# Two heads in one 32x32 product for the block between an inverse's halves

## The chip, the cores and the metric

The kernel runs on one core of one Trainium2 chip. The metric is device time in microseconds (us) for one whole execution. The engines are named as the profile names them: PE is TensorE's matrix multiply and PEld its weight load, DVE is VectorE, ACT is ScalarE, POOL is GpSimd, and SP is the engine that issues every DMA of this kernel.

## What is computed

The reference has two parts. The first is a recurrence over 768 time steps for 4 batches of 8 heads, each head with a 40x40 state. The second is a feed-forward layer over the 3072 tokens `x` that come out of it, from 320 columns to 2048 and back.

```
for t in range(S):
    ...
    y[:, :, t] = np.einsum('bhd,bhde->bhe', rt, state)
    Sa = np.einsum('bhde,bhe->bhd', state, at)
    state_decay = state * wt[:, :, None, :] - np.einsum('bhd,bhe->bhde', Sa, bt)
    state = state_decay + np.einsum('bhd,bhe->bhde', vt, kt)
...
h = x @ w_in
sp = np.maximum(h, 0.0) + np.log1p(np.exp(-np.abs(h)))
g = h * erf(sp)
return (g @ w_out).astype(np.float32)
```

## The kernel before

**Chunks and supersteps.** Time is cut into chunks of 32 steps. Inside a chunk the 32 steps of one head are solved together, which needs the inverse of a unit triangular 32x32 matrix per head and chunk. Heads are handled in two groups of 16. A superstep is 128 time steps (4 chunks) of one group, so there are 12 supersteps, numbered 0 to 11 here, and 64 such matrices in each.

**The parts of a superstep.** `prep` loads and scans the decay factors. `aphase` (once for each chunk) builds the triangular matrices with the PE step `A`, masks them on DVE and sends them to the DRAM tile `AD`. `tphase` inverts all 64 matrices of the superstep. `chain` (once for each chunk) carries the state: its PE steps are `Z`, `U`, `pmt`, `M`, `UT`, `PQ` and `Y`, and `U` needs the inverses. The feed-forward layer of the superstep before runs beside it: `mm1` is `x @ w_in`, followed by ACT and DVE work for `erf(softplus(h))`, and `mm2` is `g @ w_out`. One `mm2` step is two matmul records of the trace, one `mm1` step is eight.

**The T-phase, which the change touches.** A 32x32 unit triangular matrix is inverted by halves. The two 16x16 diagonal blocks of every matrix are loaded into the tile `Ti` and inverted there by 28 short DVE steps (`Tm`, `Ts`). The result, the inverse D of the diagonal blocks, goes to the DRAM tile `TD` by two DMAs and comes back as the tile `Tb` by four DMAs (`tb`), with each 32x32 matrix in 32 partitions and 32 columns: four matrices stand side by side in the 128 partitions and sixteen in the columns. Beside that, four DMAs (`Ap`, 64 KB each) bring the original matrices from `AD` into the tile `Ap` in the same layout. What is missing is the 16x16 block between the two halves. It comes out of D, A and D multiplied:

- `R` (DVE, L742) transposes `Tb` in blocks of 32x32 into the tile `T`
- `W` (PE, L749, four steps of sixteen 32x32 products) multiplies `Ap` with it into the PSUM bank `pA`
- `Wm` (DVE, L753) copies the bank to `T`, masked so that only the wanted 16x16 corner of each 32x32 block is left
- `DAD` (PE, L749, four steps of sixteen products) multiplies that with `Tb`
- `Tb` (DVE, L756) adds the product to the tile `Tb`

Each product is of fp32 and is two weight loads and two matmul records in the trace, so `W` is 128 matmul records in a superstep and so is `DAD`. Afterwards `U` of the next four chunks reads `Tb`.

**What sets the order.** The class `Plan` collects every step with its reads and writes. The order in which the steps are issued, and the engine of each step that has a choice (DVE, ACT or POOL), are read from two written lists, `ORDER` and `ENGINES`. Each engine executes its steps strictly in that order and waits for what a step depends on. In `ORDER` an entry of -1 or -2 is a filler matmul (L581), used at the start and at the end. There are 241 of them. SP takes its DMAs in order as well: a DMA that waits for its data holds back those behind it. `HOLD`, `ISSUE`, `PAIRS` and `COLS` are costs for a planner that runs only when the two lists do not fit the steps.

## Time and profile before

| what | value |
|---|---|
| median of 3 runs | 821.89 us |
| lowest, highest of the 3 | 817.88 us, 829.41 us |
| the profiled execution's own time | 825.36 us |
| its span, first to last instruction | 823.4 us |
| PE busy | 760.1 us (92% of the span) |
| DVE busy | 656.6 us (80%) |
| ACT busy | 609.6 us (74%) |
| POOL busy | 142.4 us (17%) |
| mean granted PE clock | 0.956 of full |

The profile is one execution. A group line names source line, engine, operation, the tiles written and read, the shapes and a count; then the busy time in us and the mean of one in ns; then the idle time of the engine just before these instructions and what ended it. A timeline line gives start and duration in us; rows of one kind that touch are merged, with their count. The end of a matmul is modelled, so a matmul row that seems long can hold a wait, and the start of the next row is the better measure. The chain of waits follows the work that ended last back to the start.

### The profile page before, as it was taken

Reading aid. Unit: us, or ns where it says so; the run is one execution under the profiler, and the core shown is the slowest. Engines: PE = TensorE matmul, PEld = TensorE weight load, DVE = VectorE, ACT = ScalarE, POOL = GpSimd, SP = SyncE. Lnnn points to the kernel's source line nnn. Section 1 sums busy time; section 2 is a strip of 40 time slices with the busy share of each in tenths; the row PEclk is TensorE's granted clock in tenths of the full one; section 3 lists DMA queues with packets and bytes.
Section 4 is the critical chain, followed back from the end, with each engine's and each line's share of the span. In section 5 each row is a group of like instructions: output and inputs, shape, how many; then the busy total and the mean of one; then the engine's idle time right before and its main releaser. Section 6 shows DMA issues by size and latency. Waiting matters only on the chain.

```text
span 823.4 us, 32379 instructions
## 1 busy us (share of the span) xinstructions
PE 760.1 (92%) x13778; PEld 588.3 (71%) x13778; DVE 656.6 (80%) x1430; ACT 609.6 (74%) x1202; POOL 142.4 (17%) x116
## 2 busy tenths in 40 slices
PE   5845998889999999999999999999899999999997
PEld 2413667657878878878877777778678777887864
DVE  6975866877889979889887978889689788778574
ACT  5453738764987878888977877878778888798882
POOL 2200321113022003011031032022123130021100
PEclk8685999889999999999998999999999999999999
DMA  8886755576666556557555546555556365313000
GB/s 253 218 218 202 182 135 145 149 167 169 145 142 166 133 146 166 146 139 176 143 157 145 143 119 158 151 142 142 136 139 153 88 162 137 69 55 94 1 17 20
DMA packets 141666, 114.60 MB, mean 139 GB/s; under 512 B 84972, under 2 KB 121964, under 8 KB 141516
## 3 DMA queue, kind: packets, MB, share of 16 engines
q1 hardware_dynamic: 141516, 112.47, 53.6%
q8 instruction: 110, 1.80, 1.0%
q14 instruction: 40, 0.33, 0.1%
HBM read 86.47 MB, written 22.02 MB: 132 GB/s over the span
## 4 chain that ended last, share of the span: by engine, by line
PE 76%; DVE 7%; DMA 6%; ACT 4%; issue 4%; SPq 1%; DVEq 0%; ACTq 0%
PE po L1067 25%; PE ph L1012 19%; PE pA L749 4%; PE gb L856 4%; PE cb L829 4%; PE pA L688 3%; PE pQ L847 3%; PE ph L581 3%; PE cb L805 2%; PE cb L796 2%; PE pQ L817 2%; PE pA L703 2%; PE gb L838 1%; PE pQ L581 1%; SPq L578 1%
## 5 line engine op out<-in xcount | busy, mean ns | idle before, releaser
L1067 PE MATMUL po<-wo,h 128*128 128x320 f32 x768 | 254.8, 456 | 1.3 <-issue 0.7
L1067 PEld LDWEIGHTS po<-wo,h 128*128 128x128 f32 x768 | 134.8, 193 | 42.5 <-issue 3.6
L1020 ACT ACTIVATE l<-l 128x512 f32<-128x512 f32 x192 | 112.2, 626 | 10.6 <-DVE nd L1045 10.1
L1012 PE MATMUL ph<-xh,wih 128*128 128x256 f32 x384 | 89.5, 314 | 0.3 <-ACT h L573 0.3
L678 POOL TENSOR_TENSOR Ab<-bk,Pr 104x512 f32<-104x512 f32 x25 | 32.9, 1318 | 275.0 <-PE pA L688 153.1
L1012 PE MATMUL ph<-xh,wil 128*128 128x256 f32 x384 | 77.4, 283 | 0.0
L1012 PE MATMUL ph<-xl,wih 128*128 128x256 f32 x384 | 77.4, 283 | 0.0
L1057 POOL TENSOR_TENSOR l<-l,r 128x512 f32<-128x512 f32 x32 | 45.2, 1420 | 174.7 <-ACT l L1020 75.3
L1058 DVE SCALAR_TENSOR_TENSOR h<-l,h 128x512 f32<-128x512 f32 x96 | 66.4, 701 | 4.4 <-POOL l L1057 2.2
L1046 DVE SCALAR_TENSOR_TENSOR r<-nd,r 128x512 f32<-128x512 f32 x96 | 66.5, 693 | 1.6 <-POOL nd L1045 0.2
L1020 ACT ACTIVATE l<-h 128x512 f32<-128x512 f32 x96 | 58.1, 627 | 12.2 <-DVE h L1058 6.0
L1012 PEld LDWEIGHTS ph<-xh,wih 128*128 128x128 f32 x384 | 61.1, 191 | 7.2 <-ACT h L573 0.4
L1045 DVE TENSOR_TENSOR nd<-l,r 128x512 f32<-128x512 f32 x76 | 53.6, 706 | 9.5 <-ACT r L1020 6.0
L1012 PEld LDWEIGHTS ph<-xh,wil 128*128 128x128 f32 x384 | 59.9, 192 | 0.0
L1012 PEld LDWEIGHTS ph<-xl,wih 128*128 128x128 f32 x384 | 59.7, 191 | 0.0
L581 PE MATMUL ph<-d 104*128 104x512 bf16 x183 | 54.2, 439 | 4.9 <-DVE d L593 4.9
L653 DVE TENSOR_TENSOR Zs<-pA,tri 64x256 f32<-64x256 f32 x96 | 40.6, 423 | 21.0 <-PE pA L688 17.7
L1020 ACT ACTIVATE r<-r 128x512 f32<-128x512 f32 x96 | 56.7, 625 | 0.5
L1020 ACT ACTIVATE r<-l 128x512 f32<-128x512 f32 x96 | 54.1, 619 | 2.8 <-DVE l L1057 1.5
L573 ACT COPY Zm<-cb 32x160 f32<-32x160 f32 x127 | 35.8, 282 | 26.7 <-PE cb L805 18.3
L1012 PE MATMUL ph<-xl,wir 128*128 128x256 f32 x192 | 54.4, 283 | 0.0
L1012 PE MATMUL ph<-xh,wir 128*128 128x256 f32 x192 | 54.3, 283 | 0.0
(135 smaller groups left out, 1528.1 us busy)
## 6 DMA issues: line engine op xcount, KB each, us to landing
vt<-in_rv_e SPq DMA_DIRECT2D x48, 416.0 KB
bk<-in_kba_e SPq DMA_DIRECT2D x45, 416.0 KB
KB<-sg SPq DMA_DIRECT2D x48, 160.0 KB
Ys<-KB SPq DMA_DIRECT2D x48, 160.0 KB
wo<-in_moe_w_in SPq DMA_DIRECT2D x10, 512.0 KB
h<-in_moe_w_out SPq DMA_DIRECT2D x10, 512.0 KB
Pr<-in_w_e SPq DMA_DIRECT2D x12, 419.7 KB
Zm<-in_v_s SPq DMA_DIRECT2D x48, 80.0 KB
```

Source lines behind the costliest of these rows:

```text
L573: self.nc.scalar.copy(o, i)
L581: self.nc.tensor.matmul((self.ph[1], self.pQ)[x], self.d1[:, :128], self.d1[:, :512], start=True, stop=True)
L653: self.P.add(name, "DVE", lambda e, x=x, xs=xs, tri=tri: nc.vector.tensor_tensor(out=o[64:128, x], in0=i[xs], in1=tri, op=ALU.mult), rd + ...
L749: nc.tensor.matmul(pw[js, i], l[js, i], r[js, i], start=True, stop=True)
L829: nc.tensor.matmul(pm[h * 64:h * 64 + 40, p], ysf[64:128, at(h, p)], zmf[64:128, p * 2 + h], start=True, stop=True)
L1012: nc.tensor.matmul(ph[:, j * 256:j * 256 + 256], a[:k, fs], b[:k], start=(m == 0), stop=(m == 7))
L1020: self.P.add(name, "ACT", lambda e: nc.scalar.activation(out=o, in_=i, **kw), rd, wr + ["act"], pr, 0.62)
L1045: P.add("nd", [("DVE", 0.69), ("POOL", 1.28)], lambda e, r=r, l=l, nd=nd: s.eng(e).tensor_tensor(out=nd, in0=l, in1=r, op=ALU.mult), [("l" ...
L1046: P.add("rho", "DVE", lambda e, r=r, nd=nd: nc.vector.scalar_tensor_tensor(out=r, in0=nd, scalar=2 * C4, in1=r, op0=ALU.add, op1=ALU.mult) ...
L1057: P.add("E", [("POOL", 1.28), ("DVE", 0.69)], lambda e: s.eng(e).tensor_tensor(out=l, in0=l, in1=r, op=ALU.mult), [("r", ir)], [("l", il)] ...
L1058: P.add("G", "DVE", lambda e: nc.vector.scalar_tensor_tensor(out=h, in0=l, scalar=-1.0, in1=h, op0=ALU.add, op1=ALU.mult), [("l", il)], [( ...
L1067: nc.tensor.matmul(po, h[:, bs], s.wo[:, f], start=(f == 0), stop=(f == 15))
```

## The change

Superstep 0 is left as it was. From superstep 1 on, only the 16x16 blocks that matter are moved and multiplied, and two heads share one 32x32 product: one head's block in the upper left 16x16 corner, the other's in the lower right, zeros elsewhere. The zeros are written once, in superstep 1, by `zAP` (a memset of the tile `Ap`, on POOL in the new list).

- The four `Ap` DMAs become eight `Np` DMAs: 16 partitions, 8 blocks and 16 columns each, so 128 runs of 64 bytes in a DMA where `Ap` has 512 runs of 128 bytes.
- Eight new DMAs `Pt` of the same size bring one 16x16 block of each D from `TD`, already in the paired layout, into the second half of the tile `Ap`. They wait for `TD`, as `tb` does.
- `R` becomes `R2`, a transpose of half as many elements. `W` becomes `W2`: four steps of eight products. `Wm` becomes `Wc`, a plain copy of half as many elements on DVE or ACT; no mask is needed. `DAD` becomes `DA2`: four steps of eight products, with `Pt`'s blocks as the right side. The last addition touches only the upper half of the columns of each block in `Tb`, so half as many elements.

Per superstep that is 64 products fewer, 128 weight loads and 128 matmul records fewer, and 12 DMAs more. The lists are new from the first entry on. They hold all steps once and 241 fillers again. `Wc` is on ACT in 5 supersteps and on DVE in 6. Other steps change engine too: in net numbers five more `nd` and five fewer `E` steps are on POOL, and five more `ysM` and four more `bTc` copies on DVE instead of ACT. The fillers and the large steps follow each other much as before. This is the order on PE from the first `W` (or `W2`) to the first `U`, by superstep, before and after:

```
 1  W*4 mm1*3 DAD*4 A mm1 bT U                                    W2*4 mm1 DA2*4 A U
 2  W*4 DAD mm2 DAD mm2*2 DAD*2 mm2 A Z mm2 bT U                  W2*4 mm2*3 DA2*4 mm2 A U
 3  W*3 mm2*2 W mm2*2 DAD mm2*2 DAD*3 mm2*2 A U                   W2 mm2 W2*3 mm2*2 DA2*4 mm2 A U
 4  W*4 mm2*4 DAD*2 mm2*2 DAD*2 mm2*2 A U                         W2 mm2 W2 mm2 W2*2 mm2*2 DA2*4 mm2 U
 5  W*3 mm2 W mm2*3 mm1 DAD*4 mm1 A U                             W2 mm2*3 W2*3 mm1 mm2 DA2*4 mm2*2 U
 6  W*3 mm2 W mm2 mm1*2 DAD*4 mm2 A U                             W2 mm2 W2*3 mm1 DA2*4 mm1 A U
 7  W mm1 W mm1*2 W*2 mm2*2 DAD*2 mm2*2 pmt DAD*2 mm2*2 A U       W2*2 mm2 W2*2 mm2*3 DA2*4 mm2*2 A U
 8  W*2 mm2 W*2 mm1*2 mm2 DAD*3 mm1 mm2 DAD mm2*2 A U             W2*4 mm1*3 mm2*2 DA2*4 mm2 A U
 9  W*4 mm1*3 DAD*2 mm2 DAD mm2 DAD mm2*2 A U                     W2*4 Z mm1*2 mm2 DA2*4 mm2*2 A mm2 U
10  W*4 mm1 mm2*4 DAD*2 mm2 DAD mm2 DAD mm2*2 A U                 W2*4 mm2*3 DA2*4 mm2*2 A U
11  W*3 mm2 W mm2*5 DAD*3 mm2*4 DAD mm2 mm1 U                     W2*4 mm2*5 DA2*4 mm2*2 U
```

And this is what SP issues in the new list from the last `TD` to the last `Pt`, by superstep:

```
 1  TD Np rv Np bw ymr Pt tb*2 Pt tb Pt*3 tb Pt*3
 2  TD zv ys tb Pt tb*2 Pt*3 xw tb xw*2 Pt xw Pt*3
 3  TD xw*2 out xw tb Pt*2 tb*3 Pt*4 xr Pt*2
 4  TD Np ys out tb Pt tb bw tb ymr tb Pt*7
 5  TD ys Np bw out tb Pt tb*2 Np tb Pt*7
 6  TD Np ys out tb Pt tb Pt*2 tb*2 bw Pt*5
 7  TD xr*4 tb*2 zs Pt tb Pt tb out Pt*6
 8  TD xr*4 tb*4 Pt*2 rv Pt*2 out Pt*4
 9  TD xr*2 tb Pt tb*2 Pt tb bw Pt*5 out Pt
10  TD Np kba Pt tb Pt tb Pt tb*2 out Pt*5
11  TD out ys Np tb Pt*2 tb*3 rv Pt*4 out Pt*2
```

The diff, without the two lists:

```diff
--- before.py
+++ after.py
 ORDER = (
...
 ENGINES = (
...
-PAIRS = dict(W=32, DAD=32, mm1=8, mm2=2, A=16, PQ=16, Z=32, U=32, M=32, Y=32, pmt=4, UT=2, bT=4, cT=1)
-COLS = dict(W=1024, DAD=1024, mm1=2048, mm2=1280, A=1024, PQ=1024, Z=1280, U=1280, M=1280, Y=1024, pmt=416, UT=256, bT=416)
-
-
-HOLD = dict(bw=0.46, tri=0.09, msk=0.09, Ap=0.37, ident=0.18, w=1.19, kba=1.2, nr=1.82, zv=0.23, ymr=0.23, rv=1.3, ys=0.46, zs=0.12, AD=0.37, Ti=0.73, TD=0.73, tb=0.37, xw=0.23, xr=0.28, out=0.46, wd=0.73)
-ISSUE = dict(ys=0.59, zs=0.83, Ti=0.58, TD=0.58, xr=0.62, tb=0.49, Ap=0.49)
-FREE = ("Am", "PQm", "MT", "Ym", "zt", "zmu", "us", "vtu", "ysM", "bTc", "ob", "hc", "Wm", "Tb", "zgb", "zcb")
+PAIRS = dict(W=32, DAD=32, W2=16, DA2=16, mm1=8, mm2=2, A=16, PQ=16, Z=32, U=32, M=32, Y=32, pmt=4, UT=2, bT=4, cT=1)
+COLS = dict(W=1024, DAD=1024, W2=512, DA2=512, mm1=2048, mm2=1280, A=1024, PQ=1024, Z=1280, U=1280, M=1280, Y=1024, pmt=416, UT=256, bT=416)
+
+
+HOLD = dict(bw=0.46, tri=0.09, msk=0.09, Ap=0.37, Np=0.1, Pt=0.1, ident=0.18, w=1.19, kba=1.2, nr=1.82, zv=0.23, ymr=0.23, rv=1.3, ys=0.46, zs=0.12, AD=0.37, Ti=0.73, TD=0.73, tb=0.37, xw=0.23, xr=0.28, out=0.46, wd=0.73)
+ISSUE = dict(ys=0.59, zs=0.83, Ti=0.58, TD=0.58, xr=0.62, tb=0.49, Ap=0.49, Np=0.45, Pt=0.45)
+FREE = ("Am", "PQm", "MT", "Ym", "zt", "zmu", "us", "vtu", "ysM", "bTc", "ob", "hc", "Wm", "Wc", "Tb", "zgb", "zcb")
 TAIL = dict(UT=0.22, pmt=0.18, bT=0.19, mm1=0.16, mm2=0.15, cT=0.15)
...
-        avj = s.AD[q % 2].rearrange("c (q j) s t -> j s (c q) t", j=4)
-        for j in range(4):
-            s.dma("Ap", lambda j=j: s.AP[j * 32:j * 32 + 32], lambda j=j: avj[j], [("ad", q % 2, c, y) for c in range(NC) for y in range(2)], [("ap", j)], pr)
+        kad = [("ad", q % 2, c, y) for c in range(NC) for y in range(2)]
+        if q == 0:
+            avj = s.AD[q % 2].rearrange("c (q j) s t -> j s (c q) t", j=4)
+            for j in range(4):
+                s.dma("Ap", lambda j=j: s.AP[j * 32:j * 32 + 32], lambda j=j: avj[j], kad, [(n, j, m) for n in ("ap", "pt") for m in range(2)], pr)
+        else:
+            if q == 1:
+                P.add("zAP", [("POOL", 0.46), ("DVE", 0.48)], lambda e: s.eng(e).memset(s.AP, 0.0), (), [(n, j, m) for n in ("ap", "pt") for j in range(4) for m in range(2)], pr)
+            avp = s.AD[q % 2].rearrange("c (a m j) s t -> j m s (c a) t", m=2, j=4)
+            for j in range(4):
+                for m in range(2):
+                    js = slice(j * 32 + m * 16, j * 32 + m * 16 + 16)
+                    s.dma("Np", lambda js=js, m=m: s.AP[js, 0:8, m * 16:m * 16 + 16], lambda j=j, m=m: avp[j, m][0:16, :, 16:32], kad, [("ap", j, m)], pr)
...
             s.dma("tb", lambda j=j: tb[j * 32:j * 32 + 32], lambda j=j: tdv[j], [("td", q % 2, x) for x in range(2)], [("tb", it, j)], pr)
         ktb = [("tb", it, j) for j in range(4)]
         fl = lambda t: t.rearrange("p a b -> p (a b)")
-        P.add("R", "DVE", lambda e: nc.vector.transpose(fl(W), fl(tb)), ktb, s.TK, pr, 0.6)
         pw = s.pA.rearrange("p (a b) -> p a b", b=32)
-
-        def mm(e, l, r, c):
-            for i in range(c * NQ, c * NQ + NQ):
+        kap = [("ap", j, m) for j in range(4) for m in range(2)]
+
+        def mm(e, o, l, r, c, n):
+            for i in range(c * n, c * n + n):
                 for j in range(4):
                     js = slice(j * 32, j * 32 + 32)
-                    nc.tensor.matmul(pw[js, i], l[js, i], r[js, i], start=True, stop=True)
-
+                    nc.tensor.matmul(o[js, i], l[js, i], r[js, i], start=True, stop=True)
+
+        if q == 0:
+            P.add("R", "DVE", lambda e: nc.vector.transpose(fl(W), fl(tb)), ktb, s.TK, pr, 0.6)
+            for c in range(NC):
+                P.add("W", "PE", lambda e, c=c: mm(e, pw, s.AP, W, c, NQ), ["T"] + kap, ["pA"], pr, 0.32)
+            P.add("Wm", "DVE", lambda e: nc.vector.tensor_tensor(out=W, in0=pw, in1=s.msk[:, None, :].to_broadcast([128, NC * NQ, 32]), op=ALU.mult), ["pA", "msk"], s.TK, pr, 0.67)
+            for c in range(NC):
+                P.add("DAD", "PE", lambda e, c=c: mm(e, pw, W, tb, c, NQ), ["T"] + ktb, ["pA"], pr, 0.32)
+            P.add("Tb", "DVE", lambda e: nc.vector.tensor_tensor(out=tb, in0=pw, in1=tb, op=ALU.add), ["pA"], ktb, pr, 0.67)
+            return
+        tdp = s.TD[q % 2].rearrange("c (a m j) s t -> j m s (c a) t", m=2, j=4)
+        for j in range(4):
+            for m in range(2):
+                js = slice(j * 32 + m * 16, j * 32 + m * 16 + 16)
+                s.dma("Pt", lambda js=js, m=m: s.AP[js, 8:16, m * 16:m * 16 + 16], lambda j=j, m=m: tdp[j, m][16:32, :, 16:32], [("td", q % 2, x) for x in range(2)], [("pt", j, m)], pr)
+        kpt = [("pt", j, m) for j in range(4) for m in range(2)]
+
+        t1 = tb.rearrange("p (a m) t -> p a m t", m=2)[:, :, :, 0:16]
+        P.add("R2", "DVE", lambda e: nc.vector.transpose(W[:, 0:8].rearrange("p a (m t) -> p a m t", m=2), t1), ktb, s.TK, pr, 0.38)
         for c in range(NC):
-            P.add("W", "PE", lambda e, c=c: mm(e, s.AP, W, c), ["T"] + [("ap", j) for j in range(4)], ["pA"], pr, 0.32)
-        P.add("Wm", "DVE", lambda e: nc.vector.tensor_tensor(out=W, in0=pw, in1=s.msk[:, None, :].to_broadcast([128, NC * NQ, 32]), op=ALU.mult), ["pA", "msk"], s.TK, pr, 0.67)
+            P.add("W2", "PE", lambda e, c=c: mm(e, pw, s.AP[:, 0:8], W[:, 0:8], c, NQ // 2), ["T"] + kap, ["pA"], pr, 0.16)
+        P.add("Wc", [("ACT", 0.4), ("DVE", 0.36)], lambda e: s.copy(e, W[:, 8:16], pw[:, 0:8]), ["pA"], s.TK, pr)
         for c in range(NC):
-            P.add("DAD", "PE", lambda e, c=c: mm(e, W, tb, c), ["T"] + ktb, ["pA"], pr, 0.32)
-        P.add("Tb", "DVE", lambda e: nc.vector.tensor_tensor(out=tb, in0=pw, in1=tb, op=ALU.add), ["pA"], ktb, pr, 0.67)
+            P.add("DA2", "PE", lambda e, c=c: mm(e, pw, W[:, 8:16], s.AP[:, 8:16], c, NQ // 2), ["T"] + kpt, ["pA"], pr, 0.2)
+        up = tb[:, :, 16:32]
+        P.add("Tb", "DVE", lambda e: nc.vector.tensor_tensor(out=up, in0=pw[:, 0:8].rearrange("p a (m t) -> p (a m) t", m=2), in1=up, op=ALU.add), ["pA"], ktb, pr, 0.42)
```

67 lines of the change are left out of this document (34 added, 33 removed), and 388 rows, old and new, of the table ORDER.

## The prediction

> **What bounds the kernel now.** I read the page's busy times first, then its chain of waits, then a table of busy time by stretch.
>
> ```profile
> span 823.4 us, 32379 instructions
> PE 760.1 (92%) x13778; PEld 588.3 (71%) x13778; DVE 656.6 (80%) x1430; ACT 609.6 (74%) x1202; POOL 142.4 (17%) x116
> PE 76%; DVE 7%; DMA 6%; ACT 4%; issue 4%; SPq 1%; DVEq 0%; ACTq 0%
> PE po L1067 25%; PE ph L1012 19%; PE pA L749 4%; PE gb L856 4%; PE cb L829 4%; PE pA L688 3%; PE pQ L847 3%; PE ph L581 3%; PE cb L805 2%; PE cb L796 2%; PE pQ L817 2%; PE pA L703 2%; PE gb L838 1%; PE pQ L581 1%; SPq L578 1%
> ```
>
> PE is busy 92% of the span and makes up 76% of the chain that ended last. L749, the line of `W` and `DAD`, is 4% of that chain. SP is 1% of it and DMA 6%. An average over the span can mislead, so I looked at four stretches of 65 us from the middle, each about one superstep long (columns: PE, PEld, DVE, ACT and POOL busy with record counts, granted clock, DMA share, GB/s).
>
> ```profile
> 190.00:255.00 65.00, 62.98 (x1330) 52.14 (x1330) 55.39 (x127) 49.17 (x101) 14.01 (x14) 1.00 0.67 162
> 255.00:320.00 65.00, 63.94 (x1319) 52.86 (x1315) 57.33 (x127) 50.67 (x104) 7.05 (x5) 1.00 0.60 151
> 320.00:385.00 65.00, 64.33 (x1287) 52.40 (x1285) 56.81 (x129) 55.44 (x113) 13.12 (x10) 1.00 0.59 149
> 515.00:580.00 65.00, 63.48 (x1183) 52.17 (x1182) 56.23 (x130) 52.84 (x107) 8.80 (x7) 1.00 0.56 145
> sum 260.00, PE 254.74 PEld 209.58 DVE 225.77 ACT 208.13 POOL 42.98; mean PE 63.68 PEld 52.39 DVE 56.44 ACT 52.03 POOL 10.74
> ```
>
> PE is busy 254.74 of 260 us there (98%) at full clock; DVE is next with 87%. So in the supersteps that the change touches PE sets the pace, and a microsecond of PE work that goes is close to a microsecond of time. The changed work is this, by group:
>
> ```profile
> L749 PE MATMUL pA<-Tb,T 32*32 32x32 f32 x1536 | 19.7, 199 | 8.9 <-issue 7.3 <-DVE T L753 1.6
> L749 PE MATMUL pA<-T,Ap 32*32 32x32 f32 x1536 | 18.3, 197 | 20.4 <-DVE T L742 15.6 <-issue 3.1 <-ACT l L1020 1.8
> L742 DVE STREAM_TRANSPOSE T<-Tb 128x512 f32<-128x512 f32 x12 | 8.5, 708 | 7.8 <-DMA Tb<-TD 7.8
> L756 DVE TENSOR_TENSOR Tb<-pA,Tb 128x512 f32<-128x512 f32 x12 | 8.3, 691 | 17.9 <-PE pA L749 17.9
> L753 DVE TENSOR_TENSOR T<-pA,msk 128x512 f32<-128x512 f32 x12 | 8.2, 687 | 10.3 <-PE pA L749 8.7 <-ACT l L1020 1.5
> ```
>
> 1536 records in 12 supersteps are 128 for `W` and 128 for `DAD`. The mean of 199 ns is a latency, four row groups overlap, so it can't be multiplied by the count.
>
> **PE work that goes.** The timeline has an undisturbed `W`, and splits of a `DAD`:
>
> ```profile
> 585.75 1.29 PE L749 MATMUL pA<-T,Ap 32*32 32x32 f32 x128
> 586.97 0.50 PE L1012 MATMUL ph<-xh,wih 128*128 128x256 f32 x2
> ...
> 655.69 0.45 PE L749 MATMUL pA<-Tb,T 32*32 32x32 f32 x32
> 656.07 0.81 PE L1067 MATMUL po<-wo,h 128*128 128x320 f32 x2
> 656.81 0.45 PE L749 MATMUL pA<-Tb,T 32*32 32x32 f32 x32
> ```
> ```profile
> 765.13 7.67 PE ph L1012 x64
> 781.62 4.31 PE po L1067 x16
> ```
>
> 128 records hold PE for 586.97 - 585.75 = 1.22 us, 9.5 ns each. `W2` and `DA2` have half the records, so a superstep saves 2 x 0.61 = 1.22 us, and 11 supersteps save 13.4 us. The Trainium skill (TensorE: Matmul & The Clock Gate, § Wait — 56ns, not 53.3ns?) has starts of matmuls never closer than about 25 ns; by that 11 x 128 records would be 35.2 us and this term 21.8 us larger. The burst above contradicts it for these four side-by-side products, so I take 13.4.
>
> The second pair shows what a break costs. From 655.69 to 656.81 are 1.12 us for 32 records of `DAD` (a quarter of 1.22, 0.305 us) and one `mm2` step, whose two records take 2 x 4.31 / 16 = 0.54 us in an unbroken run. That leaves 0.275 us for going to the small products and back. Counted in the two lists, `W` and `DAD` of supersteps 1 to 11 stand in 40 unbroken groups, `W2` and `DA2` in 28: 12 breaks fewer, 3.3 us.
>
> **Instruction delivery.** In some supersteps PE's weight loads sat idle before L749 with no releaser, which the profile calls issue:
>
> ```profile
> 185.07 0.61 PEld L749 LDWEIGHTS pA<-Tb,T 32*32 32x32 f32 x60 [1.03 <-issue]
> 477.14 0.32 PEld L749 LDWEIGHTS pA<-Tb,T 32*32 32x32 f32 x26 [1.12 <-issue]
> 593.16 0.75 PEld L749 LDWEIGHTS pA<-Tb,T 32*32 32x32 f32 x52 [2.94 <-issue]
> 595.34 0.52 PEld L749 LDWEIGHTS pA<-Tb,T 32*32 32x32 f32 x32 [0.86 <-issue]
> 597.03 0.34 PEld L749 LDWEIGHTS pA<-Tb,T 32*32 32x32 f32 x32 [0.61 <-issue]
> 656.81 0.34 PEld L749 LDWEIGHTS pA<-Tb,T 32*32 32x32 f32 x32 [0.44 <-issue]
> ```
>
> 0.44 us is the usual break (last row, priced above). What the five others have over it is 0.59 + 0.68 + 2.50 + 0.42 + 0.17 = 4.4 us. It comes where a dense burst of instructions outruns their delivery. With half the burst it can go fully or not at all; I take half, 2.2 us, bounds 0 and 4.4.
>
> **DVE and ACT.** These rows price the new steps:
>
> ```profile
> L860 DVE TENSOR_TENSOR Pr<-gb,Pr 104x256 f32<-104x256 f32 x48 | 20.2, 420 | 9.2 <-PE gb L856 8.7
> L573 ACT COPY vt<-gb 104x256 f32<-104x256 f32 x38 | 14.1, 372 | 13.7 <-PE gb L838 11.6 <-DVE nd L1045 1.3
> L575 DVE COPY vt<-gb 104x256 f32<-104x256 f32 x10 | 4.2, 422 | 2.1 <-PE gb L838 1.1 <-DMA vt<-in_rv_e 0.7
> L596 POOL MEMSET T<- 128x512 f32 x1 | 0.5, 524 | 0.3 <-POOLq L1194 0.3
> ```
>
> A superstep loses `Wm` (0.69 us of DVE); its last addition falls from 0.69 to 0.42, and `R2` lies between half of 0.71 and all of it (half taken: it handles half the elements). That is 1.31 us of DVE for each of 11 supersteps, 14.4 us, less six `Wc` on DVE at 0.42: 11.9 us. Five `Wc` put 1.9 us on ACT. DVE and ACT have 9 and 13 us of idle time in a mean stretch of 65, and PE has 1.3, so I count this at nothing. The cover is PE's own work; where it is gone, rival B has the price. `zAP`, 0.52 us on POOL (17% busy), lies ahead of the first `Np`: nothing.
>
> **The DMAs.** Twelve more issues per superstep, priced by the nearest issues and landings: two rows of SP's issues, and two from the chain of waits.
>
> ```profile
> L578 SPq DMA_DIRECT2D Ap<-AD x48: 309/474/1849, 44.1 to 687.7; - x48
> L578 SPq DMA_DIRECT2D Tb<-TD x48: 302/487/1465, 59.6 to 703.2; - x48
> 406.47 2.24 DMA Tb<-TD
> 523.78 2.11 DMA Tb<-TD
> ```
>
> At 0.47 us that is 5.6 us of SP time in a superstep. `Np` is issued around `TD` and lands long before `W2`. What can hurt is `Pt`: `DA2` waits for all eight, and behind them on SP stand the next loads of the chain (`rv`, `ys`, `zs`). In the new list the last `Pt` is 3 (superstep 1) to 10 (superstep 8) issues behind the last `tb`, mostly 6 to 8; 7 land 7 x 0.47 = 3.3 us after `tb`. Against that, between `tb` landing and `DA2` lie `R2` (0.4), `W2` (0.6) and what stands between on PE: in superstep 3 three `mm2` steps and two breaks, 1.6 + 0.6. That is 3.2 us of cover, 0.1 us less than the train. By the same count (an `mm1` step is 7.67 / 8 = 0.96 us) superstep 2 is short by 0.4 us and the others are covered with 0.1 to 1.4 us to spare; the mean cover is 3.6 us. `W2` itself has less PE work in front in superstep 2 than `W` had. I take a new wait of 1.0 us in all; bounds 0 and 0.7 us in each of eleven, 7.7. A gain below 0 I exclude, since no DMA that `DA2` or `W2` needs becomes earlier than before.
>
> **The sum.** -13.4 - 3.3 - 2.2 + 1.0 = -17.9 us. The profiled execution took 825.36 us, 1.96 more than its span, so the sum gives 807.5. The median of the runs shown is 821.89, and on that basis it is 804.0. I forecast 807 us. With the bounds (-22 to -9) on either basis the case spans 800 to 816.
>
> **Rivals.**
>
> A is the forecast, chance 0.62.
>
> B, more comes off: DVE, 87% busy in the middle, is what PE's small waits hang on, and its 11.9 us come off as well. For it speaks that `Tb <- PE` and `T <- DMA` waits put DVE and PE in a ring; against it that PE idles only 5.3 of 260 us in those stretches. 825.36 - 17.9 - 11.9 = 796. Chance 0.14.
>
> C, half the gain turns into PE waiting. The chain of waits at 404 to 416 and 515 to 536 us runs through transfers of the T-phase (the two landings above), so there PE's time is given by when `tb` lands, with up to five `Pt` now ahead of the last `tb` at 0.47 us each. 825.36 - 9 = 816. Chance 0.13.
>
> D, slower: the `Pt` train is late. If an issue takes 1.0 us instead of 0.47 (`Ap` had up to 1.85), seven take 7.0 us against the mean cover of 3.6, `DA2` waits 3.4 us, and all of PE behind it: 11 x 3.4 = 37.4. 825.36 - 18.9 + 37.4 = 844. It turns into slower than before from a wait of 1.7 us on, an issue of 0.76 us. Against it stands the median issue. The Trainium skill (DMA: Bandwidth & Descriptors, § Rules for kernel authors) speaks for it: many small transfers are to be merged, and under 64 KB a transfer is mostly overhead; here 64 KB become 8 KB. No row here shows an 8 KB transfer. Chance 0.08.
>
> E, the products were dearer than their burst shows. In superstep 0 a `DAD` starved of instructions took 75.66 - 71.24 = 4.42 us:
>
> ```profile
> 71.24 1.92 PE L749 MATMUL pA<-Tb,T 32*32 32x32 f32 x126 [0.78 <-DVE T L753]
> 75.40 0.26 PE L749 MATMUL pA<-Tb,T 32*32 32x32 f32 x2 [2.23 <-issue]
> ```
>
> If delivery ruled everywhere, 34.5 ns for each of 11 x 128 records, 48.6 us would go: 777. The five issue rows say it doesn't. By the 25 ns of the Trainium skill (TensorE: Matmul & The Clock Gate, the section above) it would be 825.36 - 35.2 = 790. Chance 0.03.
>
> **Chances and range.** Two per cent, about what a measurement of this kernel can tell from no change, lies at 805.5. Case A has 804.0 and 807.5 on its two bases, so 0.28 of its 0.62 falls below and 0.34 above. Faster: 0.28 + 0.14 + 0.03 = 0.45. Same: 0.34 + 0.13 = 0.47. Slower: 0.08. The range 794 to 822 holds A, most of B and C, and leaves out D, E and the edges of B and C, 0.19.
>
> **What would show it.** Right: L749's new lines show 704 + 128 records for each product and bursts of 64 in about 0.61 us; PE still above 97% in the middle; little waiting of L749 on `Ap<-TD`. If PE's busy time falls by 15 us and its idle time rises as much, C was right; if the `Pt` issues are near 1 us and PE waits for them at `DA2`, D; if PE's idle time between small steps shrinks too, B. A change in the start (before 127 us) or in the tail would be none of these, and would make the forecast wrong.

## The result, and the profile after

| | before | after |
|---|---|---|
| median of 4 runs each | 821.81 us | 795.47 us |
| lowest and highest | 817.88, 829.41 us | 792.24, 797.63 us |
| the profiled execution's own time | 825.36 us | 795.45 us |
| its span | 823.4 us | 793.7 us |

The changed kernel takes 0.9665 of the time before, 95% interval 0.9588 to 0.9742. That is 26.3 us by the medians and 29.7 us by the two spans: the profiled execution before lies 3.5 us above its median, the changed one at its median. The stretches below add up to the larger figure. I had forecast 807 us.

The page of the changed kernel, span, busy times and chain of waits:

```profile
span 793.7 us, 29719 instructions
PE 740.2 (93%) x12370; PEld 572.0 (72%) x12370; DVE 655.0 (83%) x1446; ACT 606.3 (76%) x1189; POOL 146.3 (18%) x114
PE 70%; DVE 12%; DMA 9%; ACT 4%; issue 3%; SPq 1%; POOL 0%; DVEq 0%; ACTq 0%
```

There are 1408 matmul records fewer (11 supersteps of 128), as the change says. PE's busy time fell by 19.9 us, which leaves 9.8 us of the gain for PE's idle time. DVE's busy time fell by only 1.6 us although the T-phase took 11.0 us from it (0.27 us at the transpose, 0.69 at `Wm` and 0.27 at the addition in each of eleven supersteps, less six `Wc` of 0.42): the new lists put other steps there. PE's share of the chain fell from 76 to 70%, and DVE's rose from 7 to 12%.

To see where the time went I divided both executions at PE's fifth and forty-eighth (last) `Z`: a start, a middle that holds what the change touches, and a tail. The rows are stretches of the span with length, then busy time and records of PE, PEld, DVE, ACT and POOL, granted clock, DMA share and GB/s. Before:

```profile
0.00:117.40 117.40, 82.97 (x1203) 46.72 (x1203) 87.84 (x183) 59.14 (x126) 22.23 (x22) 0.80 0.76 204
117.40:742.70 625.30, 601.35 (x12034) 485.81 (x12033) 515.80 (x1160) 495.64 (x990) 113.48 (x89) 0.98 0.57 141
742.70:823.40 80.70, 75.76 (x544) 55.75 (x542) 52.96 (x88) 54.86 (x87) 6.66 (x5) 0.99 0.10 30
```

And after:

```profile
0.00:107.00 107.00, 76.62 (x1196) 44.66 (x1196) 86.62 (x178) 59.77 (x126) 21.33 (x22) 0.84 0.80 222
107.00:712.60 605.60, 587.19 (x10624) 470.88 (x10623) 514.19 (x1178) 491.66 (x977) 119.13 (x88) 0.98 0.57 144
712.60:793.70 81.10, 76.38 (x553) 56.44 (x552) 54.17 (x91) 54.83 (x87) 5.85 (x4) 0.99 0.08 24
```

The start is 10.4 us shorter, the middle 19.7 us, the tail 0.4 us longer. In the middle PE's busy time fell by 14.2 us and its idle time (length less busy) from 24.0 to 18.4 us, 5.5 us less, at the same granted clock. In the start its busy time fell by 6.4 us and its idle time by 4.0, at a granted clock of 0.84 instead of 0.80. The clock differs long before superstep 0's products: from 20 to 40 us it is 0.90 where it was 0.58.

PE's waits with nothing to release them, which the profile calls issue, are the other large difference. The view of PE's waits gives the total, the count and the longest, before:

```profile
PE pA L749 <- issue: 10.4, 6, 3.1
PE cb L805 <- issue: 1.7, 2, 0.9
PE pA L688 <- issue: 1.6, 3, 0.7
PE pQ L847 <- issue: 1.1, 1, 1.1
PE gb L856 <- issue: 0.8, 1, 0.8
PE po L1067 <- issue: 0.7, 1, 0.7
PE cb L829 <- issue: 0.4, 1, 0.4
```

And after:

```profile
PE pA L695 <- issue: 0.9, 2, 0.5
PE ph L1048 <- issue: 0.5, 1, 0.5
```

From 16.7 us they fell to 1.4. By their places in the timeline, the start had 6.9 us and now has 0.9, and the middle had 9.7 and now has 0.5. L766, the new line of `W2`, `DA2` and superstep 0's `W` and `DAD`, has none (its weight loads still show 5.3 us, in twelve pieces of at most 0.44, the usual break of the prediction). In the start it is superstep 0, whose products the change leaves alone. This is its new timeline on PE:

```profile
59.92 0.65 PE L766 MATMUL pA<-T,Ap 32*32 32x32 f32 x32 [17.04 <-DVE T L769]
60.51 0.61 PE L588 MATMUL ph<-d 104*128 104x512 bf16 x1
61.04 0.65 PE L766 MATMUL pA<-T,Ap 32*32 32x32 f32 x32
61.62 0.61 PE L588 MATMUL ph<-d 104*128 104x512 bf16 x1
62.16 1.08 PE L766 MATMUL pA<-T,Ap 32*32 32x32 f32 x64
64.05 1.93 PE L766 MATMUL pA<-Tb,T 32*32 32x32 f32 x128 [0.81 <-DVE T L772]
```

`W` starts at 59.92 us (before at 64.09), has fillers (L588) after its 32nd and 64th record, and neither it nor `DAD` waits inside. Before, `DAD` waited 2.23 us for its last two records, as the prediction quotes, and `W` for its last one:

```profile
70.20 0.26 PE L749 MATMUL pA<-T,Ap 32*32 32x32 f32 x1 [3.06 <-issue]
```

The new groups of the T-phase, and one superstep's bursts in the timeline:

```profile
L766 PE MATMUL pA<-T,Ap 32*32 32x32 f32 x832 | 12.5, 201 | 18.5 <-DVE T L769 17.0 <-DVE T L785 1.3
L766 PE MATMUL pA<-Ap,T 32*32 32x32 f32 x704 | 8.4, 194 | 0.0
L785 DVE STREAM_TRANSPOSE T<-Tb 128x256 f32<-128x256 f32 x11 | 4.8, 436 | 6.7 <-DMA Tb<-TD 6.7
L792 DVE TENSOR_TENSOR Tb<-pA,Tb 128x256 f32<-128x256 f32 x11 | 4.7, 424 | 9.2 <-PE pA L766 9.1
```
```profile
170.03 0.75 PE L766 MATMUL pA<-T,Ap 32*32 32x32 f32 x64 [0.33 <-DVE T L785]
170.72 3.53 PE L1103 MATMUL po<-wo,h 128*128 128x320 f32 x6
174.17 0.75 PE L766 MATMUL pA<-Ap,T 32*32 32x32 f32 x64
174.86 0.81 PE L1103 MATMUL po<-wo,h 128*128 128x320 f32 x2
```

The counts are the forecast ones: 704 for `DA2` (`Ap,T`), and 832 (`T,Ap`) for the 704 of `W2` with the 128 of superstep 0's `W`. A burst of 64 takes 0.69 us from its start to the next row's, where I had 0.61. PE never stands at `DA2` for `Pt` (0.0 in its group). The issues on SP, with shortest, median and longest in ns:

```profile
L585 SPq DMA_DIRECT2D Ap<-AD x92: 314/429/1648, 39.1 to 674.0; - x92
L585 SPq DMA_DIRECT2D Ap<-TD x88: 303/430/1808, 113.3 to 681.2; - x88
```

`Ap<-TD` is `Pt`: 0.43 us each, not the 1.0 us of rival D.

### The profile page after: what moved, and what is told of

Read it like the earlier page. It is cut to its first block, busy times and chain, and to the rows that moved or that the text cites. A ratio compares the mean times of both kernels' runs of the same rounds, so it can differ in the third digit from the quotient of the medians.

```text
span 793.7 us, 29719 instructions
## 1 busy us (share of the span) xinstructions
PE 740.2 (93%) x12370; PEld 572.0 (72%) x12370; DVE 655.0 (83%) x1446; ACT 606.3 (76%) x1189; POOL 146.3 (18%) x114
## 4 chain that ended last, share of the span: by engine, by line
PE 70%; DVE 12%; DMA 9%; ACT 4%; issue 3%; SPq 1%; POOL 0%; DVEq 0%; ACTq 0%
PE po L1103 25%; PE ph L1048 18%; PE cb L865 4%; PE gb L892 3%; PE pQ L883 3%; PE pA L695 3%; PE ph L588 2%; PE cb L841 2%; PE pA L766 2%; PE pA L710 2%; PE cb L832 2%; PE pQ L853 2%; DMA h<-in_moe_w_out 1%; DVE l L1093 1%; DVE nd L1081 1%
## 5 line engine op out<-in xcount | busy, mean ns | idle before, releaser
L1103 PE MATMUL po<-wo,h 128*128 128x320 f32 x768 | 253.8, 455 | 2.7 <-DVE h L1094 2.5
L1103 PEld LDWEIGHTS po<-wo,h 128*128 128x128 f32 x768 | 134.5, 192 | 44.5 <-DVE h L1094 3.8
L1056 ACT ACTIVATE l<-l 128x512 f32<-128x512 f32 x192 | 112.9, 625 | 14.2 <-DVE nd L1081 11.5
L1093 POOL TENSOR_TENSOR l<-l,r 128x512 f32<-128x512 f32 x27 | 42.5, 1578 | 196.5 <-ACT l L1056 111.9
L1094 DVE SCALAR_TENSOR_TENSOR h<-l,h 128x512 f32<-128x512 f32 x96 | 69.6, 736 | 2.3 <-POOL l L1093 1.5
L1081 DVE TENSOR_TENSOR nd<-l,r 128x512 f32<-128x512 f32 x71 | 51.5, 725 | 9.9 <-ACT r L1056 6.9
L1081 POOL TENSOR_TENSOR nd<-l,r 128x512 f32<-128x512 f32 x25 | 33.6, 1343 | 139.0 <-DVE r L1082 61.1
L588 PE MATMUL ph<-d 104*128 104x512 bf16 x183 | 51.3, 420 | 3.8 <-DVE d L600 3.8
L660 DVE TENSOR_TENSOR Zs<-pA,tri 64x256 f32<-64x256 f32 x96 | 40.6, 423 | 13.1 <-PE pA L695 9.8
```

The source lines that it names most:

```text
L588: self.nc.tensor.matmul((self.ph[1], self.pQ)[x], self.d1[:, :128], self.d1[:, :512], start=True, stop=True)
L660: self.P.add(name, "DVE", lambda e, x=x, xs=xs, tri=tri: nc.vector.tensor_tensor(out=o[64:128, x], in0=i[xs], in1=tri, op=ALU.mult), rd + ...
L1056: self.P.add(name, "ACT", lambda e: nc.scalar.activation(out=o, in_=i, **kw), rd, wr + ["act"], pr, 0.62)
L1081: P.add("nd", [("DVE", 0.69), ("POOL", 1.28)], lambda e, r=r, l=l, nd=nd: s.eng(e).tensor_tensor(out=nd, in0=l, in1=r, op=ALU.mult), [("l" ...
L1093: P.add("E", [("POOL", 1.28), ("DVE", 0.69)], lambda e: s.eng(e).tensor_tensor(out=l, in0=l, in1=r, op=ALU.mult), [("r", ir)], [("l", il)] ...
L1094: P.add("G", "DVE", lambda e: nc.vector.scalar_tensor_tensor(out=h, in0=l, scalar=-1.0, in1=h, op0=ALU.add, op1=ALU.mult), [("l", il)], [( ...
```

## The experiments

All runs are compared with the kernel before on the same chip. The changed kernel's 0.9665 serves as the reference for experiments on it; 0.01 of ratio is 8.2 us. "Middle" is the same stretch as above, in the one profiled execution of each run, whose own time stands beside it. Where that time is far from the median, as in `products halved again`, the middle has to be read with care.

| run | median, us | ratio to before, 95% interval | profiled execution, us | its middle, us |
|---|---|---|---|---|
| new layout, old lists | 838.55 | 1.0148 [1.0064, 1.0232] | 842.22 | 644.5 |
| old layout, new lists | 827.49 | 1.0035 [0.9991, 1.008] | 827.97 | 634.5 |
| products twice | 838.37 | 1.0152 [1.0073, 1.0231] | 838.75 | 648.0 |
| old start, new middle | 807.0 | 0.9785 [0.9706, 0.9864] | 807.73 | 606.6 |
| products wider | 813.04 | 0.9867 [0.9794, 0.9941] | 813.89 | 622.5 |
| instructions shifted | 797.43 | 0.9686 [0.9619, 0.9752] | 797.94 | 609.1 |
| products halved again | 788.21 | 0.955 [0.9491, 0.9609] | 795.0 | 604.0 |
| `Pt` split | 827.06 | 1.0065 [1.0029, 1.0101] | 831.49 | 641.3 |
| new layout, old lists, `Np` early | 846.44 | 1.0294 [1.0255, 1.0332] | 846.29 | 645.4 |
| DVE loaded | 808.59 | 0.9834 [0.98, 0.9868] | 808.57 | 618.2 |
| new start, old middle | 832.16 | 1.0131 [1.0085, 1.0176] | 830.01 | 640.5 |
| DVE's relief alone | 822.41 | 1.0007 [0.9967, 1.0047] | 817.57 | 622.4 |

### Layout and lists apart

The changed kernel with the lists of before: each new step stands where its counterpart stood, two `Np` for each `Ap`, the eight `Pt` behind the last `tb`, `Wc` on DVE.

```diff
 ORDER = (
-    6, 27, 152, 23, 24, 7, 138, 3, 16, 159, 13, 8, 33, 4, 18, -1, 12, 0, -1, 19, 14, 22, 145, -1, 25, 21, 46, -1, -1, 1, 28, 29, -1, -1, -1, -1,
+    7, 27, 12, 25, 145, 3, 152, 21, 22, 138, 18, 0, 6, 33, 20, 23, 46, 15, 166, 4, 14, -1, 24, -1, 1, 28, 29, -1, -1, 26,
...
```

> The changed T-phase with the lists of before: each new step stands where its counterpart stood (two Np for an Ap, all eight Pt behind the last tb, Wc on DVE where Wm was). Theory (the smaller products give the gain of the middle, the lists that of the start): the start is as before (fifth Z near 117 us), no break goes, so only the 13.4 us of PE work and some of the waits on instructions go: 803 to 809 us against 821.8. Rival (the lists give nearly all of it): 815 us or more. Rival (the Pt train behind tb is not covered in the old order): DA2 waits for Pt, visible on PE at its line, and the time is 815 or more as well.

It was 1.5% slower than before, not faster. The largest of PE's waits in its middle, and the middle itself:

```profile
PE pA L734 <- DMA Ap<-AD: 10.1, 3, 3.6
```
```profile
114.90:759.40 644.50, 600.26 (x10626) 480.49 (x10625) 509.19 (x1160) 495.04 (x990) 113.63 (x89) 0.96 0.54 135
```

`W2` stands 10.1 us in three places for `Np`, which I had costed at nothing ("lands long before `W2`"). PE's idle time in the middle is 44.2 us, against 24.0 before and 18.4 with the lists that came with the change. For `Pt` it waits only 0.6 us, so that rival is out. So the layout needs an order made for it.

The row shows a second cost that I had not reckoned with. As many records as in the changed kernel hold PE 13.1 us longer (600.26 against 587.19 us), at a granted clock of 0.96 instead of 0.98. Over all fourteen profiles the two go together: where PE is idle for 39 us or more of the middle, its granted clock there is 0.96 or 0.97; where it is idle for less than 33 us, it is 0.98 or 0.99. A wait of PE thus came with more than its own length here. What sets the clock, no run here was made to show.

The other way round, the kernel before with the lists of the changed one:

```diff
 ORDER = (
-    7, 27, 12, 25, 145, 3, 152, 21, 22, 138, 18, 0, 6, 33, 20, 23, 46, 15, 166, 4, 14, -1, 24, -1, 1, 28, 29, -1, -1, 26, -1, 9, 59, -1, 10, -1,
+    6, 27, 152, 23, 24, 7, 138, 3, 16, 159, 13, 8, 33, 4, 18, -1, 12, 0, -1, 19, 14, 22, 145, -1, 25, 21, 46, -1, -1, 1,
...
```

> The T-phase of before with the new lists (the first of two Np becomes an Ap, Pt and the memset are dropped, Wm on DVE). Theory: the start is the new one (fifth Z near 107 us, 10 us gained) and W and DAD stand in 28 groups instead of 40 (3.3 us), while the PE work of the products is back: 806 to 811 us. Rival (the product gives nearly all, the start's 10 us come from fewer steps): 818 us or more. Rival (lists are all): 800 us or less.

It is as fast as the kernel before. Its start is as short as the changed kernel's to 3 us (110.1 us), and its middle is 28.9 us longer. PE waits 12.3 us for issue in that middle, 8.9 of it at the products. So neither half has the gain: it lies in the two together. Then the early `Np` (430 and 431 are the `Ti` of superstep 1, 432 is `zAP`, 433 to 440 are its `Np`) in the first of these kernels, to see whether their place in SP's queue was what slowed the old lists:

```diff
-    318, -1, 413, 399, 319, 317, 412, 262, 419, 608, -1, -1, 599, 420, 410, -1, 421, 409, 411, -1, 596, 423, -1, 417, 422, 431, 424, 430, -1, 425,
+    318, -1, 413, 399, 319, 317, 412, 262, 419, 608, -1, -1, 599, 420, 410, -1, 421, 409, 411, -1, 596, 423, -1, 417, 422, 431, 424, 430, 432, 433,
+    434, 435, 436, 437, 438, 439, 440, -1, 425, -1, -1, 418, 428, -1, -1, 257, -1, 426, -1, 263, -1, 427, -1, -1, 429, 258, -1, -1, 441, -1,
...
```

> The new T-phase in the lists of before, as in the run that took 838.55 us, with one thing changed: the eight Np loads of a superstep follow its second Ti load at once on SP, instead of standing one or two at a time where the Ap loads stood among other loads. Theory (SP's queue order made that run slow: its W2 waited 13.8 us for Np, and 1.3 us for Pt): the 13.8 us go and a little of what hung on them, 838.55 - 14 = about 825 us, 820 to 829, about the time of before, since the lists' start is still the old one (about 11 us) and Pt still stands behind the last tb. Rival (the waits on Np only show a delay that has another cause, steps that do not fit the PE order): the waiting moves to other steps, 835 to 841.

(The 13.8 us in it count one wait twice, at the matmul and at its weight load; 10.1 is right.) That made it slower still, and the theory falls in the form in which I put it; the rival gave 835 to 841, and it is over that too. The waits on `Np` are gone, and others have come:

```profile
PE gb L860 <- DMA Ym<-in_r_e: 4.3, 3, 2.9
PE cb L833 <- DMA Ys<-KB: 3.8, 1, 3.8
...
PE cb L800 <- DMA Zm<-in_v_s: 3.4, 1, 3.4
```

`Ym`, `Ys` and `Zm` are loads of the chain that now stand behind eight `Np` on SP. The middle is as long as with `Np` late (645.4 and 644.5 us), and the profiled executions are 4.1 us apart, 2.0 of it in the start; where the rest of the slowing lies is open. Twelve more issues in a superstep have to fit between the other loads, and moving them as a block moved the wait to other loads.

### Start and middle apart

The changed kernel with the old lists, fitted to it, up to the fifth `Z`, and its own from there on; and the reverse. Only the two lists differ.

```diff
 ORDER = (
-    6, 27, 152, 23, 24, 7, 138, 3, 16, 159, 13, 8, 33, 4, 18, -1, 12, 0, -1, 19, 14, 22, 145, -1, 25, 21, 46, -1, -1, 1, 28, 29, -1, -1, -1, -1,
+    7, 27, 12, 25, 145, 3, 152, 21, 22, 138, 18, 0, 6, 33, 20, 23, 46, 15, 166, 4, 14, -1, 24, -1, 1, 28, 29, -1, -1, 26,
...
```

> The changed kernel with the lists of the first experiment up to the fifth Z (the start of before) and the new lists from there on. Theory (the start's lists are worth their 10 us, and later work does not catch it up): 803 to 807 us, the fifth Z near 117 us. Rival (the middle has slack that catches a late start up): 798 us or less.

It is 0.012 of ratio, 9.9 us, slower than the changed kernel, with intervals that just overlap; by the spans 12.3 us. The start is back to 118.2 us and the middle is unchanged at 606.6. The stalls in superstep 0 are back too, inside the same products and before the same records:

```profile
63.81 1.07 PE L735 MATMUL pA<-T,Ap 32*32 32x32 f32 x63
68.24 0.26 PE L735 MATMUL pA<-T,Ap 32*32 32x32 f32 x1 [3.36 <-issue]
69.28 1.93 PE L735 MATMUL pA<-Tb,T 32*32 32x32 f32 x126 [0.78 <-DVE T L741]
73.71 0.26 PE L735 MATMUL pA<-Tb,T 32*32 32x32 f32 x2 [2.50 <-issue]
```

So some 8 to 10 us of the gain come from a new order in a part whose products did not change. The start is not the same length each time: in the five profiles with the old one it took 112.5 to 118.2 us, in the nine with the new one 106.1 to 110.1, and the two means are 8.4 us apart. The two stalls are 5.9 us here, but they are not the whole of it. Of the 11.2 us by which this start is longer than the changed kernel's, PE was busy for 9.4 and idle for 1.8: its granted clock is 0.77 against 0.84, and from 20 to 40 us 0.58 against 0.90 (0.58 to 0.67 in the five old starts, 0.86 to 0.97 in the nine new ones). What the stalls and the clock are each worth was not tried apart. The reverse:

> The new T-phase, the new lists up to the fifth Z (the start) and the lists of before, fitted to it, from there on: the complement of the run with the old start and the new middle. Theory (start and middle are independent): the run with the old lists throughout took 838.55 us, the new start is worth 11 us, so 825 to 830. Rival (the gain of the start is given back behind it when the middle is not PE-bound): 835 to 840.

This one is unclear. Its profiled span is 12.1 us below the one with the old lists throughout (828.0 against 840.1), its ratio only 0.0017, and the two intervals overlap. The spans make too much of it: the execution profiled here is the fastest of its four, the other the slowest, and the medians are 6.4 us apart. The start is 106.9 us, so the new start is short with the old middle too.

### What PE's work costs

The products of `W2` and `DA2` issued twice, so as many as before:

```diff
-            for i in range(c * n, c * n + n):
+            for i in [i for i in range(c * n, c * n + n) for _ in range(1 if q == 0 else 2)]:
```

> The changed kernel with every W2 and DA2 product from superstep 1 on issued twice over the same place, so that the number of products is that of before and all else is as changed. Theory (PE sets the pace of the middle and the work term is 13.4 us, waits on instructions 2 to 9 us more): 809 to 818 us. Rival (PE's time in the T-phase is hidden behind other engines): 797 us or less. Rival (instruction delivery rules, 34.5 ns for each record): 840 us.

This costs 0.0487, 40 us, three times the 13.4, and 838.4 us is close to the 840 of the last rival. The stretches and PE's issue waits show how it divides:

```profile
107.70:755.70 648.00, 608.43 (x12031) 489.70 (x12030) 516.21 (x1178) 492.01 (x978) 117.86 (x88) 0.97 0.54 135
```
```profile
PE pA L766 <- issue: 9.7, 9, 3.0
PE po L1103 <- issue: 5.0, 1, 5.0
PE cb L841 <- issue: 4.3, 3, 2.8
PE pA L695 <- issue: 1.6, 2, 1.1
```

The middle is 42.4 us longer: half of it is PE's busy time (608.43 - 587.19 = 21.2 us), half its idle time, and nearly all of that is issue (19.7 us). The products themselves account for 11.7 us of the busy time (22 bursts, 0.53 us each); the rest came at a granted clock of 0.97 instead of 0.98, as in the run with the old lists above. So the last rival is met in number and not in mechanism: only 9 of the 22 bursts have a wait for issue, inside or just ahead, and several of the others run through in 1.22 us. The stalls come at the products and, just behind them, at `mm2` (L1103) and `U` (L841). The Trainium skill (Runtime: NRT & Kernel Launch, § Instruction fetch mechanics) has the fetch of instructions hidden behind the pace at which they are dispatched. In this trace PE stood up to 5.0 us, in and behind dense runs of small products, with nothing else to wait for. If that wait is for the fetch, the fetch was not hidden here; that it is, no view shows.

Next, the same number of instructions, each product streaming up to four blocks instead of one:

```diff
-                    nc.tensor.matmul(o[js, i], l[js, i], r[js, i], start=True, stop=True)
+                    w = 1 if q == 0 else min(4, 8 - i)
+                    nc.tensor.matmul(o[js, i:i + w].rearrange("p a b -> p (a b)"), l[js, i], r[js, i:i + w].rearrange("p a b -> p (a b)"), start=True, stop=True)
```

> The changed kernel with each W2 and DA2 product from superstep 1 on streaming up to four blocks (128 columns, 104 on average) instead of one; the surplus is overwritten by the next products. The number of instructions is unchanged, PE time is added: by 0.84 ns for a column (an unbroken mm2 row: 4.31 us for 16 x 320 columns) and four row groups side by side, 128 records take 2.8 us instead of 1.22, 17 us in 11 supersteps. Theory (PE time costs its own length, and the surplus of the doubled products, 43 us for 13.4 us of PE work, was the delivery of instructions): 809 to 815 us, waits on issue in the middle under 3 us. Rival (any shift in time unsettles the searched lists): 825 us or more.

It costs 0.0202, 16.6 us, and PE waits for issue only 1.5 us in the middle: longer work, with no more instructions, costs its own length. And a kernel that leaves out every second product of `W2` and `DA2`:

```diff
-            for i in range(c * n, c * n + n):
+            for i in range(c * n, c * n + (n if q == 0 else n // 2)):
```

> The changed kernel with every second W2 and DA2 product from superstep 1 on left out, so the inverses of half the heads are wrong; 64 matmul records and 64 weight loads fewer in a superstep. Theory (work and number of instructions count): 6.7 us of PE work less, 786 to 790 us. Rival (the lists are fitted to where the packets begin, and fewer instructions unsettle them as more do): 795 us or more.

It gains 7.3 us by the medians and 9.5 by the ratio, as the theory said. (Its profile is of the slowest of four executions, 795.0 us, and does not show the gain.) Then the stalls: are they a matter of where the instructions happen to lie? 64 tiny products were put into PE's long wait ahead of superstep 0's `W`, which shifts all that follows by 128 instructions.

```diff
+        self.nw = getattr(self, "nw", 0) + 1
+        if self.nw == 101:
+            for _ in range(64):
+                self.nc.tensor.matmul((self.ph[1], self.pQ)[x][:, :8], self.d1[:, :128], self.d1[:, :8], start=True, stop=True)
```

> The changed kernel with 64 matmuls of 8 columns (128 instructions, half of one 16 KB instruction packet of 256) put into the PE idle time ahead of the first W. All later PE instructions sit half a packet further in their packets; no work is added behind the start. Theory (the lists are fitted to where the instruction packets begin): waits on issue in the middle grow from 0.5 us to 5 us or more, 800 to 815 us. Rival (only the number of instructions in a burst counts): 794 to 798 us.

The difference is 1.7 us, within the intervals. PE's waits for issue in the middle grow from 0.5 us to 2.6, not to 5 or more. But superstep 0's `DAD`, which ran through in the changed kernel, now waits 2.11 us for issue after its 64th record. None of the eight other profiles with the new start has such a wait, so the position of the instructions can bring a stall. One shift is little evidence for more, but the gain does not hang on one lucky position.

### Is `Pt` covered with room to spare?

Each `Pt` split in two, so 88 issues more:

```diff
-                s.dma("Pt", lambda js=js, m=m: s.AP[js, 8:16, m * 16:m * 16 + 16], lambda j=j, m=m: tdp[j, m][16:32, :, 16:32], [("td", q % 2, x) for x in range(2)], [("pt", j, m)], pr)
+                P.add("Pt", "SP", lambda e, js=js, j=j, m=m: [nc.sync.dma_start(s.AP[js, 8 + y:12 + y, m * 16:m * 16 + 16], tdp[j, m][16:32, y:y + 4, 16:32]) for y in (0, 4)], [("td", q % 2, x) for x in range(2)], [("pt", j, m)], pr, 0.45)
```

> The changed kernel with each Pt DMA split into two of four blocks, 88 issues of 0.43 us more, 3.4 us a superstep, all between TD and DA2. In the changed trace the last Pt issue ends 2.2 to 5.6 us ahead of DA2, and a landing takes about 2.2 us. Theory (the train is covered by a hair, so each further issue is waited for): 11 waits of 0 to 3.4 us, about 22 us in all, 810 to 822 us, seen at the T-phase line as idle time ended by DMA Ap<-TD. Rival (PE would have waited for other things anyway): 800 us or less.

It takes the whole gain away, and more than either theory said: 0.04, 32.9 us. SP's own issue became part of the chain of waits, and PE now waits for `Pt` and for DVE. The chain, the two waits and the middle:

```profile
PE 47%; DVE 17%; DMA 14%; SPq 11%; ACT 6%; issue 4%; POOL 1%; DVEq 0%; POOLq 0%; ACTq 0%
```
```profile
PE pA L766 <- DMA Ap<-TD: 7.9, 10, 1.5
PE pA L766 <- DVE T L785: 7.8, 6, 2.7
```
```profile
106.90:748.20 641.30, 597.74 (x10624) 478.02 (x10623) 515.03 (x1178) 491.94 (x978) 117.85 (x88) 0.97 0.54 136
```

The median issue of a half is 0.424 us, as long as a whole `Pt`, so 88 of them are 37 us of SP time, 3.4 in a superstep, of which 0.79 us show at `DA2` in each of ten places. The middle is 35.7 us longer: 25.2 us of PE's idle time, and 10.6 us in which the same 10624 records hold PE longer, again at a clock of 0.97 instead of 0.98. My theory counted only the waits at `DA2`.

### What DVE's time is worth

The changed kernel with three transposes more behind the last addition of each T-phase, whose results nobody reads:

```diff
-        P.add("Tb", "DVE", lambda e: nc.vector.tensor_tensor(out=up, in0=pw[:, 0:8].rearrange("p a (m t) -> p (a m) t", m=2), in1=up, op=ALU.add), ["pA"], ktb, pr, 0.42)
+        P.add("Tb", "DVE", lambda e: [nc.vector.tensor_tensor(out=up, in0=pw[:, 0:8].rearrange("p a (m t) -> p (a m) t", m=2), in1=up, op=ALU.add)] + [nc.vector.transpose(W[:, 0:8].rearrange("p a (m t) -> p a m t", m=2), t1) for _ in range(3)], ["pA"], ktb, pr, 0.42)
```

> The changed kernel with three transposes more behind the last addition of every T-phase from superstep 1 on, whose results nobody reads: 3 x 0.43 x 11 = 14 us of DVE time put back, about what the change takes from DVE. Rival B (DVE's relief comes off in full): 795.5 + 14 = 807 to 811. Case A (DVE's relief is worth nothing while PE's own work covers it): 795 to 799. In between, some part of what DVE is given stands in PE's way: the addition is followed by steps that U and the next A wait for.

It costs 0.0169, 13.9 us, about all of what was put in (DVE's busy time in the middle grew by 15.5 us). The middle, and one of PE's waits:

```profile
107.30:725.50 618.20, 588.99 (x10623) 471.73 (x10622) 529.72 (x1211) 491.65 (x978) 117.09 (x88) 0.98 0.57 141
```
```profile
PE pA L710 <- DVE Zs L660: 4.4, 6, 1.7
```

PE has 1.8 us more of busy time and 10.8 us more of idle time. `A` (L710) waits 4.4 us for the mask step `Zs` that stands behind the transposes on DVE. In the changed kernel that row reads:

```profile
PE pA L710 <- DVE Zs L660: 0.4, 1, 0.4
```

So DVE, with 85% of the middle busy (514.19 of 605.6), had no slack at this place. Then the mirror image, the kernel before, lists unchanged, with the shorter DVE steps alone:

```diff
+        hb = 16 if q == 0 else 8
-        P.add("R", "DVE", lambda e: nc.vector.transpose(fl(W), fl(tb)), ktb, s.TK, pr, 0.6)
+        P.add("R", "DVE", lambda e, hb=hb: nc.vector.transpose(fl(W[:, 0:hb]), fl(tb[:, 0:hb])), ktb, s.TK, pr, 0.6)
...
```

> The kernel before, its lists and products unchanged, in which from superstep 1 on the transpose, the masked copy and the last addition handle only the first eight of the sixteen blocks of a partition; so the rest of the blocks between the halves is not computed rightly, and this kernel leaves work out. DVE loses (0.708 - 0.436) + (0.687 - 0.42) + (0.691 - 0.424) = 0.81 us in each of eleven supersteps, 8.9 us, all of it between the landing of tb and U. The run with 14 us of DVE put back into the changed kernel cost 13 to 14 us. If DVE is such a price in the lists of before too (rival B as recorded): 8.9 us faster than before, ratio 0.987 to 0.991. If an order written for the longer steps gives the gain to waits elsewhere (case A's count at nothing): within 2 us of before, ratio 0.997 to 1.001.

Nothing came of it: 1.0007, and the interval excludes neither 3 us of gain nor 4 of loss, but excludes 8.9. DVE's time in the same middle fell as it should:

```profile
112.50:734.90 622.40, 597.59 (x12034) 483.40 (x12033) 505.64 (x1160) 495.81 (x991) 112.22 (x89) 0.99 0.57 142
```

515.80 - 505.64 = 10.2 us less for DVE, and PE's idle time is 24.8 us where it was 24.0. So taking 10 us from DVE gained nothing in the old order, and giving it 14 us in the new one cost them in full. Case A was right on the first, and the second is what rival B was about. The two runs differ in the order and in the place of the DVE steps, and no run puts the three transposes into the kernel before; which of the two makes the difference is not shown.

## Why the prediction was right or wrong

**What bounds the kernel: right.** PE sets the pace in the middle. It is busy 601.35 of 625.3 us before and 587.19 of 605.6 after, 97% of the changed one, and the run with longer products paid 16.6 us for the 17 expected.

**The work term, -13.4 us: right in kind, a little too large.** A burst of 64 holds PE 0.69 us and not 0.61. With 1.22 for 128, that makes 0.53 us saved by each, 11.7 us for 22 of them. With the 3.3 us for breaks that is 15.0 us, and PE's busy time in the middle fell by 14.2. The breaks alone were not tried, so their 3.3 us stay an estimate.

**Instruction delivery, -2.2 us: the term that was mis-sized in the middle.** I counted only L749's rows in the weight loads, 4.4 us, and took half. In the middle PE's matmuls waited 9.7 us for issue, 5.1 of it at L749 and 4.6 at other steps (0.7 right behind one of its bursts), and 9.2 of it went. The two crossed runs divide this. In the old lists the new layout still waits 6.6 us, 1.9 at its products and 4.7 elsewhere; in the new lists the old layout waits 12.3 us, 8.9 at its products and 3.4 elsewhere. So at the products the smaller bursts took off 3.2 us in the old order, within my bounds (0 and 4.4), and all in the new one. The waits elsewhere, which I had left out, went only where layout and order came together. The run with the products issued twice put 19.7 us of such waits back. Whether the wait is one for delivery at all, no view shows.

**`Pt`, +1.0 us: right within its bounds.** No wait at `DA2` shows (0 and not 1.0 us), and an issue takes 0.43 us. The cover is as thin as I reckoned: twice the issues cost 32.9 us. Of the page's rule that I named for rival D (the Trainium skill, DMA: Bandwidth & Descriptors, § Rules for kernel authors), the run with `Pt` split bears out the direction, since a half costs SP as much as a whole; but 8 KB at 0.43 us cost no more to issue than the 64 KB `Ap` before at 0.474.

**`Np` at nothing: right for the new lists alone.** In the old lists they cost PE 10.1 us at `W2`, and moved ahead, as much at other loads.

**DVE's relief at nothing: right as a step, wrong as a conclusion on DVE.** Alone it gave nothing. But the new lists spent it: they put other steps on DVE (busy 655.0 us where it was 656.6) and run it with 85% of the middle busy where it had 82%, and 14 us put back cost 13.9. With as much DVE work put back, this order is at 808.6 us. How much of the 26 us a searched order would have found without it is open.

**The start, not in the sum at all.** I had written that a change there would be none of my terms and would make the forecast wrong, and that is where 10.4 of the 29.7 us lie. The run with the old start puts 9.9 us of it back; the 8.4 us between the mean starts is the safer figure. Part of the evidence was in the profile: 3.06 and 2.23 us of issue in superstep 0, the second of which I quoted for rival E, and a granted clock of 0.58 from 20 to 40 us. I treated the start as given because its products are unchanged, though I had noted that the lists are new from the first entry on.

**The sum of the middle.** -14.2 (work and breaks) - 9.2 (issue) + 3.4 (other waits: DVE 1.5, DMA 1.1, ACT 0.8 by PE's idle rows in the timeline) = -20.0, against -19.7 measured and -17.9 forecast; the 0.3 us left are gaps too short for a row. So case A was the right case for the middle, and on the basis of the profiled execution what separates 807.5 from 795.5 is nearly all the start. That the middle came within 1.8 us owes something to luck, since errors cancel: 7.0 us more went from issue than forecast, against 2.5 us less from work and breaks (16.7 forecast) and 2.4 us more in new waits. The bounds that I gave as -22 to -9 add up to -21.1 and -9.0, and the middle lies inside them; the whole gain does not.

**The rivals.** B's 796 is nearest to the measured time, but by luck and not by its mechanism: DVE's relief alone gave nothing. C (PE's gain turned into waiting) didn't happen; PE's idle time fell. D's mechanism shows in the run with `Pt` split, and the new lists stay on its safe side. E's stalled products are there in superstep 0 and in the run with twice the products, but were not the rule before.

None of the kernels that compute everything is faster than the changed one.
